# Doubles made into floats with three VectorE passes and a scaled copy, instead of four passes, a magnitude and a PSUM bank

## The chip, the cores and the metric

One core of a Trainium2 chip runs the whole program. The metric is device time in microseconds (us), the median of several executions; the profile is of one more execution. TensorE multiplies matrices, VectorE and GpSimd work elementwise, ScalarE applies functions and copies, and SyncE only issues DMAs. The profile calls them PE (with PEld for its weight loads), DVE, POOL, ACT and SP. Each engine takes its instructions strictly in the order of the program.

## The reference

An attention with a state that is corrected at every step feeds two layers of a feed-forward network. Cut to what matters here:

```
B, H, S, D = 4, 8, 768, 48              # q, k, v in float32
for t in range(S):
    y[t] = q[t] @ state
    state += beta[t] * outer(k_n[t], v[t] - k_n[t] @ state)
x = y as 3072 tokens of 384
h = x @ w_in;  g = P(h) / Q(h);  x = g @ w_out       # first MLP, 384 -> 2048 -> 384
h = x @ w_in2; g = h * tanh(softplus(h)); out = g @ w_out2
```

All four weight matrices arrive as float64. [...]

## The kernel before

**Stages.** The attention runs in chunks of 64 tokens, 12 of them (`u`), in pairs; then come 96 units of the first MLP and 96 of the second. A unit is one token group of 512 with one block of 128 of the 2048 hidden features: 9 matmuls up (L818), an elementwise chain, and 9 or 12 matmuls down (L904, L937).

**Attention.** For each chunk `prepare` loads, normalizes and transposes k and q and makes masked Gram matrices (L374 on DVE). For each pair of chunks `inverse` inverts 32 x 32 triangles in 30 steps of a product (L449) and a sum (L455): it opens with a transposition on DVE (L437) and a scaling (L440), and closes with a scaling (L459) and a transposition on DVE (L462) that writes `xt`. Four of the six inverses (chunks 3, 5, 7, 11) run on POOL, the other two (1 and 9, the first and the fifth) on DVE. `step` is the recurrence: matmuls of the pair (L509, L526, L541, L549, L564) in turns with subtractions on DVE (L517) and copies on ACT. Its L526 reads `xt`, so the recurrence of a pair starts when that pair's inverse is done.

**Weights.** `Weights.convert` makes one half of a feature block (384 doubles in each of 128 partitions) into a high and a low float32r part: 64 conversions, of which 32 (first MLP) run beside the attention, 16 in the middle of the first MLP and 16 at the start of the second. One conversion is a DMA of the doubles to `w64` (called `w` in the rows), `mag` (L665, ACT, the magnitude of the high words, to `wm`; in the second MLP L661 on DVE instead), `size` (L670 clips and L674 shifts and masks the exponent, on DVE), `sign` (L680) and `low` (L686), both on DVE, a rounding copy `out` (L693, ACT) and the remainder `rest` (L698, POOL). What the passes between read and write lies in a PSUM bank called `word` during the attention, in the `r` bank of PSUM (left over from the first MLP) in the second MLP, and in `wm` itself, in SBUF, during the first MLP.

**What sets the order.** In the attention all engines' orders are written by `Plan`: every piece of work is added with its engine, an assumed duration in ns, and the buffers it reads and writes; a list scheduler with 800 random trials of priorities picks the shortest order that it finds. The times in it are not seen by the chip, only the order is. Where the plan leaves TensorE without work it writes matmuls of zeros (`heat`, L1046) into TensorE's order, as many as the gap holds. In the two MLPs the order is written by hand in `MLP_OPS`, and `Conv.pull` deals out the steps of the conversions between units, one of `size`, `sign` and `low` at a time.

Of the kernel before, what the change touches and what calls it, by code (L numbers as in the profile page):

```python
# [9 lines left out]
F32 = mybir.dt.float32  # L10
F32R = mybir.dt.float32r
I32 = mybir.dt.int32
I64 = mybir.dt.int64
ACTF = mybir.ActivationFunctionType
ALU = mybir.AluOpType
# [7 lines left out]
TOK = 512  # L23
# [145 lines left out]
class Attention:  # L169
# [4 lines left out]
    def __init__(self, ctx, tc, q, k, v, beta, x1, spare):  # L174
        nc = self.nc = tc.nc
        self.x1 = x1
        B, H, S, D = q.shape
        self.B, self.H, self.D = B, H, D
        self.NU = S // C
        self.M = B * H // 2  # L180
        self.DP = 64
        M, DP, NU = self.M, self.DP, self.NU

        big = ctx.enter_context(tc.tile_pool(name="a_big", bufs=1))
        ps = ctx.enter_context(tc.tile_pool(name="a_ps", bufs=1, space=PSUM))

        def ring(name, n, shape, pool=big):
            return [pool.tile(shape, F32, name=f"{name}{i}") for i in range(n)]

        self.ident, = ring("ident", 1, [128, 128])  # L190
        self.mask, = ring("mask", 1, [128, 2 * C])
        self.beta, = ring("beta", 1, [128, NU // 2, HC])
        self.kn = ring("kn", self.NKN, [128, M, DP])
        self.qn = ring("qn", self.NQ, [128, M, DP])
        self.v = ring("v", self.NV, [128, M, D])
        self.kq = ring("kq", self.NT, [128, 2, M // 2, 128])
        self.gm = ring("gm", self.NT, [128, M, HC + C])
        self.su = ring("su", 2, [128, 2, M // 2, D])
        self.u = ring("u", 1, [128, M, D])
        self.r2, = ring("r2", 1, [128, M, D])  # L200
        self.lg = ring("lg", 1, [128, 2, M, HC])
        self.xs = ring("xs", 2, [128, HC, HC])
        self.lg.append(spare.rearrange("p k t -> p (k t)")[:, 0:2 * M * HC].rearrange("p (u m t) -> p u m t", u=2, m=M))
        self.xt = ring("xt", 3, [128, 2 * M, HC])
        self.tmp = ring("tmp", 2, [128, 256])
        self.yst = ring("yst", 1, [128, M, GU * C])
        self.nrm = [{n: t for n, t in zip(("ss", "n0", "r0", "n1", "ri"), ring(f"nrm{i}_", 5, [128, 2, M]))} for i in range(2)]
        self.word, = ring("word", 1, [128, 384], ps)
        self.s_all, = ring("s_all", 1, [128, 2, TOK], ps)
        self.s_ps = [self.s_all[:, i] for i in range(2)]  # L210
        self.c_ps = ring("c_ps", 2, [128, TOK], ps)
        self.t_ps = ring("t_ps", 2, [128, TOK], ps)
        self.y_ps, = ring("y_ps", 1, [128, TOK], ps)
        self.banks = 0

        def heads(t):
            t = t.rearrange("b h s d -> (b h) s d").rearrange("(a c n) s d -> a c s n d", a=2, c=2)
            return [[t[a, c] for c in range(2)] for a in range(2)]

        self.kv, self.qv, self.vv = heads(k), heads(q), heads(v)  # L220
        bv = beta.rearrange("b h s -> (b h) s").rearrange("(a m) (g u c t) -> a c u m g t", a=2, u=2, c=2, t=HC)
        self.bv = [bv[n // 4, n // 2 % 2, n % 2] for n in range(8)]
# [400 lines left out]
class Weights:  # L623
# [2 lines left out]

    LEAST = 2.0 ** -15
    MOST = 1.875 * 2.0 ** 16  # L630
    free = False
    word = None

    def __init__(self, nc, w_in, w_out, sb, kept, passing, scratch):
        self.nc, self.sb, self.kept, self.scratch = nc, sb, kept, scratch
# [10 lines left out]
    def convert(self, f, side):  # L646
        nc = self.nc
        w = {}

        def get():  # L650
            w["raw"] = self.sb.tile([128, 3, 128], I64, "w64")
            src = self.w_out[f * 128:(f + 1) * 128] if side else self.w_in[:, :, f * 128:(f + 1) * 128]
            nc.sync.dma_start(out=w["raw"], in_=src)

        def word(i):
            return w["raw"].rearrange("p k c -> p (k c)").bitcast(I32).rearrange("p (n t) -> p n t", t=2)[:, :, i]

        def mag():
            w["m"] = self.sb.tile([128, 384], I32, "wm")
            if self.free:  # L660
                nc.vector.tensor_scalar(  # L661
                    out=w["m"], in0=word(1), scalar1=0x7FFFFFFF, scalar2=None, op0=ALU.bitwise_and
                )
            else:
                nc.scalar.activation(out=w["m"].bitcast(F32), in_=word(1).bitcast(F32), func=ACTF.Abs)  # L665

        def size():
            m = w["m"]
            w["x"] = m if self.word is None else self.word.bitcast(I32)
            nc.vector.tensor_scalar(  # L670
                out=w["x"].bitcast(F32), in0=w["m"].bitcast(F32), scalar1=self.LEAST, scalar2=self.MOST,
                op0=ALU.max, op1=ALU.min,
            )
            nc.vector.tensor_scalar(  # L674
                out=w["x"], in0=w["x"], scalar1=3, scalar2=0x3FFFFFF8,
                op0=ALU.logical_shift_left, op1=ALU.bitwise_and,
            )

        def sign():
            nc.vector.scalar_tensor_tensor(  # L680
                out=w["x"], in0=word(1), scalar=-(1 << 30), in1=w["x"],
                op0=ALU.bitwise_and, op1=ALU.bitwise_or,
            )

        def low():
            nc.vector.scalar_tensor_tensor(  # L686
                out=w["m"], in0=word(0), scalar=29, in1=w["x"],
                op0=ALU.logical_shift_right, op1=ALU.bitwise_or,
            )

        def out():
            m = w["m"].bitcast(F32).rearrange("p (k c) -> p k c", k=3)
            nc.scalar.copy(out=self.tile(f)[:, 0, side], in_=m)  # L693

        def rest():
            t = self.tile(f)
            m = w["m"].bitcast(F32).rearrange("p (k c) -> p k c", k=3)
            nc.gpsimd.tensor_tensor(out=t[:, 1, side], in0=m, in1=t[:, 0, side].bitcast(F32), op=ALU.subtract)  # L698

        def done():  # L700
            if side and f in self.tag:
                self.store(f)

        return get, mag, size, sign, low, out, rest, done

    def plan(self, p, fs):

        slots = len(self.kept)
        for i, f in enumerate(fs):
            slot, late = f"w{i % slots}", LATE * i - AHEAD  # L710
            for side in range(2):
                n = 2 * i + side
                get, mag, size, sign, low, out, rest, _ = self.convert(f, side)
                raw, m = f"w64{n % 2}", f"wm{n % 2}"
                p.add("SP", 1500, get, (), [raw], more=2500, early=late)
                p.add("ACT", 560, mag, [raw], [m], early=late)
                p.add("DVE", 1160, size, [m], ["word"], early=late)
                p.add("DVE", 570, sign, [raw], ["word"], early=late)
                p.add("DVE", 570, low, [raw, "word"], [m], early=late)
                p.add("ACT", 500, out, [m], [slot], early=late)  # L720
                p.add("POOL", 1000, rest, [m], [slot], early=late)
            if f not in self.kept:
                p.add("SP", 2500, lambda f=f: self.store(f), [slot], (), more=2500, early=late)
# [224 lines left out]
def tile_delta_attention_two_mlps(  # L948
# [14 lines left out]
    nc = tc.nc  # L963
# [15 lines left out]
    ps = Ring()  # L979
# [14 lines left out]
    w1 = Weights(nc, moe_w_in, moe_w_out, sb, range(FQ), (), wd[0])  # L994
    w2 = Weights(nc, moe2_w_in, moe2_w_out, sb, (), range(DIRECT), wd[1])
# [37 lines left out]
    with ExitStack() as actx:  # L1033
        m1.xr[0] = sb.tile([128, 3, TOK], F32, "xraw")
        at = Attention(actx, tc, q, k, v, beta, x1, m1.xr[0])
# [4 lines left out]
        nc.scalar.activation(out=ab[:, 4:6], in_=ab[:, 4:6], func=ACTF.Abs)  # L1040
        zero = actx.enter_context(tc.tile_pool(name="zero", bufs=1)).tile([128, 128], F32, name="zero")
        nc.gpsimd.memset(zero, 0.0)
        w1.word = at.word

        def heat(used=False):
            nc.tensor.matmul(  # L1046
# [10 lines left out]
        late = 20000  # L1057
# [11 lines left out]
    with ExitStack() as bctx:  # L1069
# [22 lines left out]
        for i in range(n2 + max(LG.values())):  # L1092
# [10 lines left out]
            for op in LISTS[kind]:  # L1103
# [19 lines left out]
                elif op == "fw" and i in fetch_w:  # L1123
                    fetch, f = fetch_w[i]
                    fetch(f)
                elif op == "fx" and i + 8 < n2 and starts(i + 8):
                    mlp(i + 8).fetch_x(units[i + 8][0])
                elif op == "xa":
                    at_x(lambda m: m.x_hi)
                elif op == "xB":  # L1130
                    at_x(lambda m: lambda g, k: m.x_lo(g, k, "V"))
                elif op == "c" and i > n1:
                    w2.free = True
                    w2.word = w2.word or ps.tile([128, TOK], F32, "r")[:, 0:384]
                    conv.pull(CONV_RATE)
                elif op == "c" and i in calm:
                    conv.pull(6 * DIRECT * (calm.index(i) + 1) // len(calm) - conv.n)
                elif op == "f":
                    conv.flush()
# [29 lines left out]
```

## Time and profile before

| | us |
|---|---|
| median of 3 runs | 1139.59 (1138.97 to 1141.21) |
| span of the profiled execution | 1133.3 |
| of it: attention, to the first matmul of the first MLP | 0 to 317.1 |
| first MLP | 317.1 to about 718 |
| second MLP | about 718 to 1133.3 |

The profile gives the span from the first to the last instruction of its execution and no other time of it; the median of the runs is 6.3 us longer than this span. Over the span PE is busy 94%, DVE 64%, ACT 54% and POOL 47%, but these are means over three stages with different limits: DVE is busy 93% of the first MLP and 28% of the second, and POOL works in the attention, the first MLP and the first eighth of the second. So the rows further down are taken stage by stage. A busy time is the time in which an engine has an instruction under way; the idle time before an instruction is put down to what ended it.

### The profile page before, as it was taken

To read this page: it belongs to the slowest core of one execution; us is meant where nothing else is said; L and a number is where in the kernel's file an instruction comes from. 1 tells how busy PE (TensorE), PEld (TensorE's weight loads), DVE (VectorE), ACT (ScalarE), POOL (GpSimd) and SP (SyncE) were. 2 spreads that over 40 slices of the span, in tenths; PEclk is the share of its full clock that TensorE was granted. 3 is DMA by queue.
4 is the path that set the end of the run, shared out by engine and by line. 5 is a ranking of instruction groups with operands and counts; after the bars stand their busy time and mean duration, and the time that the engine had idled before them with its cause. 6 is when DMAs were issued, how large, how long until landed. Compare 5 with 4: busy or idle time off the path is not lost.

```text
span 1133.3 us, 25035 instructions
## 1 busy us (share of the span) xinstructions
PE 1068.1 (94%) x10354; PEld 933.0 (82%) x10354; DVE 720.1 (64%) x1206; ACT 611.6 (54%) x1101; POOL 538.2 (47%) x623
## 2 busy tenths in 40 slices
PE   5899899888879999999999999999999999999998
PEld 4888888778768778787887878899999998999997
DVE  5878475995669999999999999993121211212110
ACT  4415445334368888888888888743323323333322
POOL 3188878476347777787777777773000000000000
PEclk9989899988999999999999999999999999999999
DMA  7428676326585031121202036150101001010000
GB/s 139 90 54 201 163 190 172 85 59 197 178 305 204 4 108 43 50 77 52 100 17 98 14 126 249 45 190 6 56 1 56 1 1 57 1 56 1 29 1 28
DMA packets 121265, 99.23 MB, mean 88 GB/s; under 512 B 79808, under 2 KB 104512, under 8 KB 121152
## 3 DMA queue, kind: packets, MB, share of 16 engines
q1 hardware_dynamic: 120896, 97.54, 28.8%
q8 instruction: 81, 1.33, 0.5%
q14 instruction: 32, 0.26, 0.1%
q0 software_dynamic: 256, 0.10, 0.1%
HBM read 66.16 MB, written 31.46 MB: 86 GB/s over the span
## 4 chain that ended last, share of the span: by engine, by line
PE 54%; POOL 15%; ACT 11%; DVE 9%; issue 7%; DMA 2%; SPq 2%; POOLq 0%; DVEq 0%; ACTq 0%
PE h L818 21%; PE o L937 18%; POOL q L861 8%; PE o L904 4%; POOL gh L833 3%; ACT r L868 3%; POOL r L851 3%; PE y_ps L564 3%; PE c_ps L526 3%; ACT q L848 2%; ACT r L870 2%; DVE tmp L449 2%; PE c_ps L541 1%; PE c_ps L509 1%; PE s_all L549 1%
## 5 line engine op out<-in xcount | busy, mean ns | idle before, releaser
L818 PE MATMUL h<-x,w 128*128 128x512 f32 x1728 | 429.1, 393 | 7.5 <-DVE s L877 3.5
L818 PEld LDWEIGHTS h<-x,w 128*128 128x128 f32 x1728 | 321.3, 188 | 76.6 <-DVE s L877 8.7
L833 DVE TENSOR_TENSOR gh<-g,gh 128x512 fp32r<-128x512 f32 x80 | 55.4, 693 | 283.0 <-ACT g L928 274.3
L904 PE MATMUL o<-gh,w 128*128 128x512 f32 x864 | 213.5, 391 | 4.9 <-ACT ev L1026 4.9
L937 PE MATMUL o<-w,gh 128*128 128x384 f32 x1152 | 216.9, 337 | 0.0
L937 PEld LDWEIGHTS o<-w,gh 128*128 128x128 f32 x1152 | 204.7, 188 | 8.1
L904 PEld LDWEIGHTS o<-gh,w 128*128 128x128 f32 x864 | 161.7, 188 | 41.0 <-ACT ev L1026 7.8
L923 ACT ACTIVATE gh<-h 128x512 fp32r<-128x512 f32 x96 | 57.6, 600 | 229.0 <-PE h L818 229.0
L833 POOL TENSOR_TENSOR gh<-g,gh 128x512 fp32r<-128x512 f32 x112 | 145.1, 1296 | 23.9 <-ACT g L928 21.4
L861 POOL TENSOR_TENSOR q<-q,r 128x512 f32<-128x512 f32 x96 | 124.6, 1298 | 65.7 <-ACT r L855 61.2
L868 ACT ACTIVATE r<-q,cst 128x512 f32<-128x512 f32 x96 | 66.4, 691 | 52.5 <-POOL q L861 52.5
L884 DVE SCALAR_TENSOR_TENSOR q<-q,r 128x512 f32<-128x512 f32 x96 | 65.2, 679 | 15.0 <-ACT r L870 14.7
L698 POOL TENSOR_TENSOR w<-wm,w 128x384 fp32r<-128x384 f32 x48 | 49.6, 1035 | 52.6 <-ACT w L693 52.4
L857 ACT ACTIVATE s<-h,ab 128x512 f32<-128x512 f32 x96 | 74.3, 774 | 0.0
L877 DVE SCALAR_TENSOR_TENSOR s<-s,ab,h 128x512 f32<-128x512 f32 x96 | 71.8, 748 | 3.4
L888 DVE SCALAR_TENSOR_TENSOR r<-s,ab,r 128x512 f32<-128x512 f32 x96 | 71.7, 746 | 0.0
L875 DVE TENSOR_TENSOR s<-s,h 128x512 f32<-128x512 f32 x96 | 65.4, 681 | 6.0 <-ACT s L857 6.0
L893 DVE SCALAR_TENSOR_TENSOR g<-q,r 128x512 f32<-128x512 f32 x96 | 65.9, 687 | 3.3
L455 POOL TENSOR_TENSOR xs<-xs,tmp 128x30 f32<-128x30 f32 (+14 forms) x120 | 62.1, 518 | 9.4
L449 POOL TENSOR_TENSOR tmp<-xs 128x30 f32<-128x30 f32 (+14 forms) x120 | 58.3, 486 | 7.0
L829 ACT CAST gh<-g 128x512 fp32r<-128x512 f32 x96 | 59.7, 622 | 0.0
L851 POOL TENSOR_SCALAR r<-q,ab 128x512 f32<-128x512 f32 x54 | 42.1, 780 | 34.8 <-ACT q L848 34.8
(125 smaller groups left out, 1397.0 us busy)
## 6 DMA issues: line engine op xcount, KB each, us to landing
w<-w SPq DMA_DIRECT2D x36, 768.0 KB, 7.3
w<-in_moe_w_in_dram SPq DMA_DIRECT2D x32, 384.0 KB, 4.0
w<-in_moe_w_out_dram SPq DMA_DIRECT2D x32, 384.0 KB, 3.4
xraw<-x SPq DMA_DIRECT2D x36, 256.0 KB, 3.9
w<-wt SPq DMA_DIRECT2D x8, 768.0 KB, 3.8
kn<-in_k_dram SPq DMA_DIRECT2D x48, 96.0 KB, 3.7
qn<-in_q_dram SPq DMA_DIRECT2D x48, 96.0 KB, 3.4
v<-in_v_dram SPq DMA_DIRECT2D x48, 96.0 KB, 3.5
```

The lines of the kernel that those rows point to most:

```text
L449: eng.tensor_tensor(out=tv, in0=ls[:, j, j + 1:HC].unsqueeze(1).to_broadcast([128, j, n]), in1=xs[:, 0:j, j:j + 1].to_broadcast([128, j, n ...
L818: self.nc.tensor.matmul(out=self.st[i]["h"], lhsT=self.w.t[f][:, a, 0, k], rhs=self.x[g][:, b, k], start=(n == 0), stop=(n == 8),)
L833: (nc.gpsimd if engine == "P" else nc.vector).tensor_tensor(out=s["gh"][:, 1], in0=s["g"], in1=s["gh"][:, 0].bitcast(F32), op=ALU.subtract)
L851: nc.gpsimd.tensor_scalar(out=s["r"], in0=s["q"], scalar1=k["b1"], scalar2=k["b0"], op0=ALU.mult, op1=ALU.add)
L857: nc.scalar.activation(out=s["s"], in_=s["h"], func=ACTF.Identity, scale=k["a3"], bias=k["a2"])
L861: nc.gpsimd.tensor_tensor(out=s["q"], in0=s["q"], in1=s["r"], op=ALU.mult)
L868: nc.scalar.activation(out=s["r"], in_=s["q"], func=ACTF.Ln, bias=k["c"])
L877: nc.vector.scalar_tensor_tensor(out=s["s"], in0=s["s"], scalar=k["a1"], in1=s["h"], op0=ALU.add, op1=ALU.mult)
L888: nc.vector.scalar_tensor_tensor(out=s["r"], in0=s["s"], scalar=k["a0"], in1=s["r"], op0=ALU.add, op1=ALU.mult)
L893: nc.vector.scalar_tensor_tensor(out=s["g"], in0=s["q"], scalar=2.0, in1=s["r"], op0=ALU.subtract, op1=ALU.mult, reverse0=True)
L904: self.nc.tensor.matmul(out=self.acc[g][d], lhsT=self.w.t[f][:, a, 1, d], rhs=self.st[i]["gh"][:, b], start=(first and n == 0), stop=(last ...
L937: self.nc.tensor.matmul(out=self.acc[g][t][:, 0:384], lhsT=self.st[i]["gh"][:, a, t * 128:(t + 1) * 128], rhs=self.w.t[f][:, b, 1].rearran ...
```

## The change

`mag` becomes a scaled copy: ACT multiplies the high word, read as a float, by 2^-112, which moves the exponent by the difference of the two formats' biases and keeps the sign (in the second MLP DVE does the same with a multiplication). `size` is then one shift by three to the left, from `wm` into the high words of the raw doubles themselves, nothing is clipped and nothing masked; `sign` takes the sign bit from `wm`, and `low` is as it was. The bank `word` and the use of the `r` bank fall away: all that the three passes read and write is in SBUF, in every stage. In the plan `size` is entered with 360 instead of 1160 ns, and the buffers that the passes claim are named anew.

```
-        self.word, = ring("word", 1, [128, 384], ps)
...
-    LEAST = 2.0 ** -15
-    MOST = 1.875 * 2.0 ** 16
+    SCALE = 2.0 ** -112
...
         def mag():
             w["m"] = self.sb.tile([128, 384], I32, "wm")
+            m, src = w["m"].bitcast(F32), word(1).bitcast(F32)
             if self.free:
-                nc.vector.tensor_scalar(
-                    out=w["m"], in0=word(1), scalar1=0x7FFFFFFF, scalar2=None, op0=ALU.bitwise_and
-                )
+                nc.vector.tensor_scalar(out=m, in0=src, scalar1=self.SCALE, scalar2=None, op0=ALU.mult)
             else:
-                nc.scalar.activation(out=w["m"].bitcast(F32), in_=word(1).bitcast(F32), func=ACTF.Abs)
+                nc.scalar.activation(out=m, in_=src, func=ACTF.Copy, scale=self.SCALE)
 
         def size():
-            m = w["m"]
-            w["x"] = m if self.word is None else self.word.bitcast(I32)
+            w["x"] = word(1)
             nc.vector.tensor_scalar(
-                out=w["x"].bitcast(F32), in0=w["m"].bitcast(F32), scalar1=self.LEAST, scalar2=self.MOST,
-                op0=ALU.max, op1=ALU.min,
-            )
-            nc.vector.tensor_scalar(
-                out=w["x"], in0=w["x"], scalar1=3, scalar2=0x3FFFFFF8,
-                op0=ALU.logical_shift_left, op1=ALU.bitwise_and,
+                out=w["x"], in0=w["m"], scalar1=3, scalar2=None, op0=ALU.logical_shift_left
             )
 
         def sign():
             nc.vector.scalar_tensor_tensor(
-                out=w["x"], in0=word(1), scalar=-(1 << 30), in1=w["x"],
+                out=w["x"], in0=w["m"], scalar=-(1 << 31), in1=w["x"],
                 op0=ALU.bitwise_and, op1=ALU.bitwise_or,
             )
...
-                p.add("DVE", 1160, size, [m], ["word"], early=late)
-                p.add("DVE", 570, sign, [raw], ["word"], early=late)
-                p.add("DVE", 570, low, [raw, "word"], [m], early=late)
+                p.add("DVE", 360, size, [m], [raw], early=late)
+                p.add("DVE", 570, sign, [m], [raw], early=late)
+                p.add("DVE", 570, low, [raw], [m], early=late)
```

The new costs make the scheduler write another order for the whole attention. In the changed program `size` is L665, `sign` L670 and `low` L676, `rest` L688, and other lines of the attention stand one lower than before (L436 for L437, L461 for L462, L516 for L517, L525 for L526), `heat` is L1035. The conversions keep their places in the orders of the two MLPs, one pass shorter each. Three places:

DVE ahead of the transposition that opens the first inverse (`yst<-lg`), the program before:

```order
L374 TENSOR_TENSOR gm_138<-c_ps_169,mask_120 128x384
L670 TENSOR_SCALAR word_166<-wm 128x384
L674 TENSOR_SCALAR word_166<-word_166 128x384
L680 SCALAR_TENSOR_TENSOR word_166<-w_351,word_166 128x384
L686 SCALAR_TENSOR_TENSOR wm<-w_351,word_166 128x384
L670 TENSOR_SCALAR word_166<-wm 128x384
L674 TENSOR_SCALAR word_166<-word_166 128x384
L437 STREAM_TRANSPOSE yst_155<-lg_147 128x1024
```

and the changed one:

```order
L373 TENSOR_TENSOR gm_138<-c_ps_168,mask_120 128x384
L316 TENSOR_REDUCE nrm_0_156<-gm_142 128x16
L326 TENSOR_SCALAR nrm_0_156<-nrm_0_156 128x32
L436 STREAM_TRANSPOSE yst_155<-lg_147 128x1024
L373 TENSOR_TENSOR xraw<-t_ps_170,mask_120 128x128
L373 TENSOR_TENSOR xraw<-t_ps_169,mask_120 128x128
L373 TENSOR_TENSOR gm_139<-t_ps_170,mask_120 128x384
L373 TENSOR_TENSOR gm_139<-t_ps_169,mask_120 128x384
L665 TENSOR_SCALAR w_450<-wm 128x384
```

One and a half conversions went from ahead of the first inverse to behind it, and two sums of squares (L316) with a small L326 came forward.

DVE at the end of the fifth inverse, which it runs itself (`xs_148` to `xt_151`), the program before:

```order
L517 TENSOR_TENSOR r_146<-r_146,c_ps_168 128x384
L449 TENSOR_TENSOR tmp_153<-xs_148 128x84
L455 TENSOR_TENSOR xs_148<-xs_148,tmp_153 128x28x3
L449 TENSOR_TENSOR tmp_153<-xs_148 128x58
L455 TENSOR_TENSOR xs_148<-xs_148,tmp_153 128x29x2
L670 TENSOR_SCALAR word_166<-wm 128x384
L674 TENSOR_SCALAR word_166<-word_166 128x384
L449 TENSOR_TENSOR tmp_153<-xs_148 128x30
L455 TENSOR_TENSOR xs_148<-xs_148,tmp_153 128x30
L459 TENSOR_TENSOR xs_148<-xs_148,beta_121 128x1024
L462 STREAM_TRANSPOSE xt_151<-xs_148 128x32x32
```

and a piece of the changed one, a little further ahead in the same inverse:

```order
L454 TENSOR_TENSOR xs_148<-xs_148,tmp_153 128x23x8
L676 SCALAR_TENSOR_TENSOR wm<-w_3442 128x384
L448 TENSOR_TENSOR tmp_153<-xs_148 128x168
L454 TENSOR_TENSOR xs_148<-xs_148,tmp_153 128x24x7
L448 TENSOR_TENSOR tmp_153<-xs_148 128x150
L454 TENSOR_TENSOR xs_148<-xs_148,tmp_153 128x25x6
L516 TENSOR_TENSOR r_146<-v_130,c_ps_168 128x384
L676 SCALAR_TENSOR_TENSOR wm<-w_3524 128x384
L448 TENSOR_TENSOR tmp_153<-xs_148 128x130
L454 TENSOR_TENSOR xs_148<-xs_148,tmp_153 128x26x5
```

Conversions moved forward, into this inverse: between the transposition that closes the fourth inverse (L462, `xt_150`) and the one that closes the fifth there are 2 passes of conversions before and 10 now.

PE where the recurrence of the fifth pair begins (its first L526 that reads `xt_151`), the program before:

```order
L564 MATMUL y_ps_172<-kq_132,su_144 48x64 x16
L509 MATMUL c_ps_168<-su_143,kq_133 64x48 x16
L564 MATMUL y_ps_172<-gm_138,u_145 48x64 x16
L526 MATMUL c_ps_169<-r_146,xt_151 32x48 x16
L526 MATMUL c_ps_168<-r_146,xt_151 32x48 x16
```

and the changed one:

```order
L563 MATMUL y_ps_171<-gm_138,u_145 48x64 x16
L508 MATMUL c_ps_167<-su_143,kq_133 64x48 x16
L563 MATMUL y_ps_171<-kq_133,su_143 48x64 x16
L1035 MATMUL s_all_166<-ident_119,zero 128x128 x24
L525 MATMUL c_ps_168<-r_146,xt_151 32x48 x16
L525 MATMUL c_ps_167<-r_146,xt_151 32x48 x16
```

24 matmuls of zeros now stand ahead of it, where there were none.

## Rows read from the trace of the kernel before

**Rows 1.** Busy us of each engine in stretches: start:end, length, engine (instructions), clock.
```profile
core 0: us, PE busy (x) PEld busy (x) DVE busy (x) ACT busy (x) POOL busy (x), PEclk, DMA share, GB/s
217.50:254.00 36.50, 30.65 (x935) 28.39 (x936) 34.30 (x63) 10.59 (x21) 20.48 (x36) 0.91 0.19 47
254.00:287.60 33.60, 28.49 (x907) 26.63 (x904) 20.04 (x36) 12.90 (x27) 20.99 (x34) 0.85 0.59 171
317.10:717.90 400.80, 389.27 (x1691) 315.35 (x1692) 373.65 (x554) 343.07 (x582) 298.77 (x258) 1.00 0.28 101
717.90:1133.30 415.40, 410.62 (x2055) 371.11 (x2053) 116.01 (x183) 136.89 (x259) 44.15 (x38) 1.00 0.11 36
```
**Rows 2.** PE's waits, 317 to 720 us: us in total, times, longest.
```profile
PE o L904 <- ACT ev L1026: 4.9, 5, 1.4
PE h L818 <- DVE s L877: 3.5, 6, 1.7
PE h L818 <- DVE q L884: 3.0, 1, 3.0
```
**Rows 3.** Passes of conversions by line: ns min/median/max, first and last start.
```profile
L674 DVE TENSOR_SCALAR wm<-wm x16: 359/708/1061, 352.6 to 681.2; 128x384 int32<-128x384 int32 x16
L661 DVE TENSOR_SCALAR wm<-w x15: 347/564/1494, 726.9 to 770.1; 128x384 int32<-128x384 int32 x15
L680 DVE SCALAR_TENSOR_TENSOR word<-w,word x32: 503/561/578, 31.2 to 315.9; 128x384 int32<-128x384 int32 x32
L680 DVE SCALAR_TENSOR_TENSOR wm<-w,wm x16: 551/690/1359, 356.3 to 684.8; 128x384 int32<-128x384 int32 x16
L686 DVE SCALAR_TENSOR_TENSOR wm<-w,wm x16: 642/920/1358, 364.3 to 688.7; 128x384 int32<-128x384 int32 x16
```
**Rows 4.** Timeline (start, us, instruction) of POOL and DVE where both read SBUF.
```profile
227.76 2.43 POOL L440 TENSOR_TENSOR xs<-xs,beta 128x1024 f32<-128x1024 f32 x1 [13.03 <-DVE xs L437]
228.01 2.45 DVE L455 TENSOR_TENSOR xs<-xs,tmp 128x238 f32<-128x238 f32 x1
...
406.74 1.30 POOL L833 TENSOR_TENSOR gh<-g,gh 128x512 fp32r<-128x512 f32 x1 [0.37 <-ACT gh L829]
407.09 1.36 DVE L680 SCALAR_TENSOR_TENSOR wm<-w,wm 128x384 int32<-128x384 int32 x1
```
**Rows 5.** Timeline of POOL, the same two steps in its first and its last inverse.
```profile
61.53 0.41 POOL L449 TENSOR_TENSOR tmp<-xs 128x130 f32<-128x130 f32 x1
72.68 0.60 POOL L449 TENSOR_TENSOR tmp<-xs 128x238 f32<-128x238 f32 x1
...
233.88 0.41 POOL L449 TENSOR_TENSOR tmp<-xs 128x130 f32<-128x130 f32 x1
245.25 0.61 POOL L449 TENSOR_TENSOR tmp<-xs 128x238 f32<-128x238 f32 x1
```
**Rows 6.** POOL: a remainder and the third inverse's closing (timeline), its longest waits, 27:317.
```profile
34.84 1.00 POOL L698 TENSOR_TENSOR w<-wm,w 128x384 fp32r<-128x384 f32 x1 [4.34 <-ACT w L693]
...
212.82 1.91 POOL L459 TENSOR_TENSOR xs<-xs,beta 128x1024 f32<-128x1024 f32 x1
...
POOL w L698 <- ACT w L693: 50.6, 16, 7.6
```
**Rows 7.** Chain of waits: start, us, piece; DVE up to the opening of POOL's first inverse.
```profile
53.13 0.40 DVE tmp L449
...
53.96 1.88 DVE xs L437
```
**Rows 8.** PE where the fifth pair begins (timeline), and its matmuls of zeros (groups).
```profile
256.43 1.55 PE L526 MATMUL c_ps<-r,xt 32*32 32x48 f32 x64 [1.87 <-DVE r L517]
...
L1046 PE MATMUL s_all<-ident,zero 128*128 128x128 f32 x158 | 21.3, 288 | 0.0
```
**Rows 9.** Timeline of PE at the start of the first MLP.
```profile
317.13 4.42 PE L818 MATMUL h<-x,w 128*128 128x512 f32 x18 [0.90 <-DVE wm L686]
...
331.40 2.34 PE L818 MATMUL h<-x,w 128*128 128x512 f32 x9 [1.75 <-DVE s L877]
```

More of the change, by code (lines that the diff above doesn't have):

```diff
@@ L623 @@
 class Weights:
-    LEAST = 2.0 ** -15
-    MOST = 1.875 * 2.0 ** 16
+    SCALE = 2.0 ** -112
     free = False
-    word = None
     def __init__(self, nc, w_in, w_out, sb, kept, passing, scratch):
@@ L1042, in tile_delta_attention_two_mlps @@
         nc.gpsimd.memset(zero, 0.0)
-        w1.word = at.word
         def heat(used=False):
@@ L1133, in tile_delta_attention_two_mlps @@
                     w2.free = True
-                    w2.word = w2.word or ps.tile([128, TOK], F32, "r")[:, 0:384]
                     conv.pull(CONV_RATE)
```

## The prediction

> **What bounds the kernel now.** I read the busy time by stretches first [rows 1], because the three stages have different limits. In the second MLP PE is busy 410.6 of 415.4 us and DVE 116.0: only PE counts there. In the first MLP PE is busy 389.3 of 400.8 us, but DVE is close behind with 373.7, so the next view is what PE waited for in that stage [rows 2]: 4.9 us on ACT's copies of accumulators, 6.5 us in seven waits on DVE. No more than these can a faster DVE give back there. In the attention no engine is full: between the closing of the fourth and of the fifth inverse (217.5 to 254.0 us) DVE is busy 34.3 of 36.5 us, and in the next stretch 20.0 of 33.6 [rows 1]. So the attention is bound by a chain that changes engines: POOL's inverses one after the other, DVE's own fifth inverse, and the recurrence on PE, which may start a pair only when its `xt` is there. The conversions are not in that chain by themselves. They count by where they stand in DVE's and POOL's order, and by what they do to the instructions beside them.
>
> **What a pass costs now and then.** Before, four passes with an operand in PSUM take 0.56 us each and never over 0.58 (L680 on `word` [rows 3]), 2.24 us for a conversion. Afterwards three passes lie wholly in SBUF, as they did in the first MLP, where the same kinds have medians of 0.71, 0.69 and 0.92 us, together 2.32, and minima of 0.36, 0.55 and 0.64, together 1.55 [rows 3]. The cause stands in the timeline: a DVE instruction with both inputs in SBUF started 0.25 us after POOL's 2.43 us scaling and took 2.45 us, and an L680 beside a POOL subtraction took 1.36 us [rows 4]. Such a DVE instruction ends only after POOL's has ended. In the attention POOL's instructions are shorter (0.41 to 0.61 us [rows 5]) but come one behind the other. I take 2.1 us for a conversion, nearer to the medians; the bounds are 1.55 and 2.32. So DVE is relieved by 0.1 us for each of the 32 conversions of the attention, while the new plan counts on 1.50 us for it, 0.74 less than the 2.24. The shift also writes every second word; the one row with that stride (L661, reading it) has 0.35 us at least [rows 3], and were it slower, up to 0.56 us, it would stay inside these bounds.
>
> **(a) The start.** Up to the opening of POOL's first inverse (53.96 us, straight behind steps of DVE's first inverse [rows 7]) DVE has 6 passes before and 1 afterwards, but 2 more inverse steps of two times 0.40 us and one small instruction of about 0.2 us: -6 x 0.56 + 0.36 + 1.6 + 0.2 = **-1.2 us**. At best the 3.4 us of the passes, at worst 0.
>
> **(b) POOL's queue.** From the opening of its first inverse to the closing of its third, POOL runs 18 remainders before and 20 afterwards; each takes 1.00 us [rows 6]: +2.0 us. What the passes in SBUF cost POOL the trace doesn't show for 384 elements. Nearest: the same nine steps of an inverse took 11.15 us with DVE in PSUM (61.53 to 72.68) and 11.37 beside DVE's own steps of some 200 elements (233.88 to 245.25) [rows 5], 0.22 us more for about 17 DVE instructions. 20 conversions with two two-input passes each lie between 0.5 us by that and 22 us if POOL waits 0.55 us each time; the passes are twice as long as those steps, so I take 0.05 us each, +2.0 us. POOL's waits for conversions (50.6 us in 16 waits [rows 6]) I leave as they are: the DVE part of a conversion hardly shortens. Together **+4.0 us** (-6 to +22).
>
> **(c) The fifth pair.** Between the closings of the fourth and the fifth inverse DVE was full [rows 1], and it gets 8 passes more: 8 x 0.36 to 0.92 = +2.9 to +7.4 us. PE shows the same from its side: it waited 1.87 us for that inverse [rows 8], and its order now holds 24 matmuls of zeros there; 79 of them took 21.3 us [rows 8] (the row counts each twice), 0.27 us each, so 6.5 us, which PE runs whether it would have to wait or not. 6.5 - 1.9 = **+4.6 us**. In the whole attention 20 more are in the order (253, not 233).
>
> **(d) The end of the attention.** Behind the last inverse 6 passes stand on DVE and 4 remainders on POOL, where 26 and 8 stood. So the first matmul of the first MLP no longer waits 0.9 us for the last conversion [rows 9], and DVE's subtractions in the last pair meet fewer passes: another 1.0 us (0 to 3). **-1.9 us.** What is late next is the recurrence itself, which PE's own matmuls fill.
>
> **(e) The MLPs.** In the first MLP 16 passes of 0.71 us leave DVE, 11.3 of its 373.7 us. PE can get back at most its waits on DVE, and of their 6.5 us the one of 3.0 and the longest of the others, 1.75 at 331.4 us [rows 2, 9], come ahead of the first conversion there (its L674 from 352.6 us [rows 3]). Of the 1.7 us left I take half: **-0.8 us** (0 to -1.7). In the second the passes leave PSUM, and beside POOL's subtractions they will take about the 2.3 us that four took: DVE has the same load, and PE reads a block's weights only some units after they are made. Cost 0; without that cover some 2 us.
>
> ACT's scaled copy reads and writes what the magnitude did: nothing.
>
> **The sum.** -1.2 + 4.0 + 4.6 - 1.9 - 0.8 = +4.7 us on the span of 1133.3, so 1138.0; with the 6.3 us between the span and the median of the runs, **1144.3 us**.
>
> **Rivals.** *The passes run free.* If most of them find POOL idle (it does idle, 50.6 us, for these very conversions [rows 6]), each comes in 1.55 us, and remainders arrive up to 0.7 us sooner: 16 waits x 0.7 = 11 us, of which I count 8; with (a) -1.2, two remainders +2, (c) +4.6, (d) -3.9 and (e) -1.7 that is -8.2: 1131.4 us. For it: a shift right behind POOL's instruction can take 0.36 us. Against: the medians of the first MLP, and 24 fixed matmuls in PE's order.
>
> *The terms cancel.* The six passes at the start come through whole (-3.4), the port costs POOL nothing (+2.0 for two remainders), (c) to (e) as above: +0.5, 1140.1 us.
>
> *POOL is held for whole passes.* Slower by far: each of the three passes keeps POOL's next instruction waiting for its own length, 20 x (0.36 + 0.55 + 0.55) = 29 us up to the third inverse. POOL's waits for conversions would hide about half of it; with +15 for the 2.0 of the port the sum is +17.7: 1157.3 us. It decides once POOL's cadence in an inverse stretches by more than 0.2 us at a pass; rows 5 speak against it, with shorter DVE instructions. The Trainium skill, "SBUF — State Buffer", section "Who interferes with whom", states this rule: VectorE with two SBUF inputs, or in a two-port mode, and GpSimd exclude each other for a whole instruction, and the one that comes second blocks fully. By that rule this rival is the forecast, at 1157.3 us; rows 4 agree for a DVE that comes second, rows 5 show hardly any cost to POOL.
>
> **How the numbers follow.** The forecast has 0.42, the free passes 0.28, the cancelling 0.22, the held POOL 0.08. 0.2%, or 2.3 us, is about what a measurement of this kernel can tell from no change. Faster: 0.28 and a little of the cancelling, 0.30. Slower: the held POOL and most of the forecast, 0.47. The same: 0.23. The forecast alone runs from 1140 to 1152 (port 0.5 to 8 us, (c) 2.9 to 7.4). The range for 8 in 10 leaves out the held POOL and the far end of the free passes: 1131 to 1152.
>
> **What would show it.** Passes in the attention with medians near 0.7 us, not 0.4 to 0.55; POOL's third inverse closing 2 to 5 us later than at 214.7 [rows 6]; the first L526 of the fifth pair behind 24 fills or later; the first MLP starting at about 319 us, not 317.1, without a wait on a conversion, and lasting about 1 us less. It would be wrong if the opening of POOL's first inverse moved by much more than 1 us, if POOL's waits for conversions fell by half, or if TensorE's clock (0.91 and 0.85 in two stretches [rows 1]) rose or fell with the new order.

## The result, and the profile after

| | before | after |
|---|---|---|
| median, same chip, 4 executions each | 1139.28 us (1137.06 to 1141.21) | 1150.05 us (1145.61 to 1150.47) |
| ratio, 95% interval | | 1.0106 (1.0069 to 1.0143) |
| span of the profiled execution | 1133.3 us | 1148.6 us |
| first matmul of the first MLP | 317.1 us | 332.9 us |
| from there to the end | 816.2 us | 815.7 us |

The changed kernel is slower, by 1.1% in the ratio and by 10.8 us, or 0.9%, between the medians. A ratio, here and below, is of the fast executions alone (those within 1.5% of the fastest of their kernel) and is not the quotient of the medians beside it. The two profiled spans lie 15.3 us apart, and all of it is in the attention. In runs that give both numbers the time is about 2 us longer than the span, not 6.3, so the execution profiled before lies some 4 us under its median.

Stretches of the changed kernel, columns as in [rows 1]. The first two lie between the closing transpositions of the fourth and fifth, and of the fifth and sixth inverse; then the two MLPs.

```profile
232.90:275.70 42.80, 35.50 (x1018) 33.51 (x1016) 40.42 (x73) 15.66 (x32) 26.01 (x40) 0.92 0.47 132
275.70:304.80 29.10, 25.30 (x814) 24.39 (x814) 14.89 (x24) 11.14 (x24) 20.57 (x32) 0.77 0.54 160
...
332.90:733.00 400.10, 389.24 (x1690) 316.12 (x1690) 368.67 (x538) 343.08 (x581) 296.85 (x257) 1.00 0.28 101
733.00:1148.60 415.60, 410.93 (x2056) 371.14 (x2054) 122.80 (x167) 136.58 (x260) 47.77 (x38) 1.00 0.11 36
```

Against [rows 1] the DVE-bound stretch has grown from 36.5 to 42.8 us, the one behind it has shrunk from 33.6 to 29.1, and the MLPs have kept their lengths.

What four passes cost in the attention before and what three cost now: groups by line, 27 us to the end of the attention (busy us in all, mean ns of one | idle before them), first before, then after.

```profile
L674 DVE TENSOR_SCALAR word<-word 128x384 int32<-128x384 int32 x32 | 18.1, 566 | 1.1
L680 DVE SCALAR_TENSOR_TENSOR word<-w,word 128x384 int32<-128x384 int32 x32 | 17.9, 558 | 0.7
L670 DVE TENSOR_SCALAR word<-wm 128x384 f32<-128x384 f32 x32 | 17.8, 556 | 28.4 <-ACT wm L665 27.8
L686 DVE SCALAR_TENSOR_TENSOR wm<-w,word 128x384 int32<-128x384 int32 x32 | 17.7, 554 | 2.7
```

```profile
L670 DVE SCALAR_TENSOR_TENSOR w<-wm,w 128x384 int32<-128x384 int32 x32 | 27.5, 859 | 1.0
L676 DVE SCALAR_TENSOR_TENSOR wm<-w 128x384 int32<-128x384 int32 x32 | 24.6, 774 | 1.4
L665 DVE TENSOR_SCALAR w<-wm 128x384 int32<-128x384 int32 x32 | 20.3, 633 | 15.4 <-ACT wm L661 15.2
```

Four passes took 71.5 us of DVE, three take 72.4. A quarter of the instructions is gone and none of the time: 2.27 us for a conversion, where the plan now counts 1.50 (360, 570 and 570 ns).

The same hold-up from POOL's side: the products and sums of its four inverses, groups as above, before and after.

```profile
L455 POOL TENSOR_TENSOR xs<-xs,tmp 128x30 f32<-128x30 f32 (+14 forms) x120 | 62.1, 518 | 9.4
L449 POOL TENSOR_TENSOR tmp<-xs 128x30 f32<-128x30 f32 (+14 forms) x120 | 58.3, 486 | 7.0
```

```profile
L454 POOL TENSOR_TENSOR xs<-xs,tmp 128x30 f32<-128x30 f32 (+14 forms) x120 | 67.8, 565 | 9.4
L448 POOL TENSOR_TENSOR tmp<-xs 128x30 f32<-128x30 f32 (+14 forms) x120 | 65.3, 544 | 7.0
```

The same 240 instructions (120 steps of a product and a sum) take 133.1 us, not 120.4. The timeline of the changed kernel (start, us, instruction, in brackets what was waited for) shows one place, in the order of time, ahead of the third inverse's end:

```profile
209.86 0.56 ACT L661 ACTIVATE wm<-w 128x384 f32<-128x384 f32 x1 [3.02 <-DMA w<-in_moe_w_in_dram]
...
210.45 0.36 DVE L665 TENSOR_SCALAR w<-wm 128x384 int32<-128x384 int32 x1 [2.02 <-ACT wm L661]
...
210.85 0.56 DVE L670 SCALAR_TENSOR_TENSOR w<-wm,w 128x384 int32<-128x384 int32 x1
...
212.51 0.35 DVE L341 RECIPROCAL nrm<-nrm 128x32 f32<-128x32 f32 x1
...
213.00 3.02 POOL L393 TENSOR_TENSOR kn<-kn,nrm 128x768 f32<-128x768 f32 x2 [3.39 <-DVE nrm L341]
...
213.42 1.27 DVE L665 TENSOR_SCALAR w<-wm 128x384 int32<-128x384 int32 x1
...
214.73 1.71 DVE L670 SCALAR_TENSOR_TENSOR w<-wm,w 128x384 int32<-128x384 int32 x1
...
225.99 1.91 POOL L458 TENSOR_TENSOR xs<-xs,beta 128x1024 f32<-128x1024 f32 x1
```

Two things are to be seen. DVE stood 2.02 us at a conversion whose doubles had not landed; behind that pass in its order came the norm (L341), for which POOL waited 3.39 us with its inverse unfinished. That is order. Then a shift and a sign pass, begun 0.4 and 1.7 us after POOL's two scalings began, took 1.27 and 1.71 us instead of 0.36 and 0.56. That is the place of the operands. The closing of the third inverse is at 225.99 us; in [rows 6] it is at 212.82.

And the fifth pair on PE (timeline), answering [rows 8]:

```profile
267.82 3.62 PE L1035 MATMUL s_all<-ident,zero 128*128 128x128 f32 x31
277.75 2.53 PE L525 MATMUL c_ps<-r,xt 32*32 32x48 f32 x58 [6.30 <-DVE xt L461]
...
332.85 4.42 PE L808 MATMUL h<-x,w 128*128 128x512 f32 x18
340.34 5.03 PE L808 MATMUL h<-x,w 128*128 128x512 f32 x14 [3.07 <-DMA w<-w]
```

The matmuls of zeros were over by 271.4 us (the first row shows only the last 31 of their 48 records, two to a matmul); PE then waited 6.30 us for the fifth inverse itself. The first MLP no longer waits for a conversion [rows 9], but later for a fetched weight.

### The profile page after: what moved, and what is told of

Its sections match the earlier page's. It is cut to its first block, busy times and chain, and to the rows that moved or that the text cites. A ratio compares the mean times of both kernels' runs of the same rounds, so it can differ in the third digit from the quotient of the medians.

```text
span 1148.6 us, 25024 instructions
## 1 busy us (share of the span) xinstructions
PE 1077.8 (94%) x10394; PEld 945.3 (82%) x10394; DVE 721.4 (63%) x1142; ACT 611.4 (53%) x1101; POOL 554.6 (48%) x623
## 4 chain that ended last, share of the span: by engine, by line
PE 46%; POOL 17%; DVE 12%; ACT 12%; issue 8%; DMA 3%; SPq 2%; POOLq 0%; DVEq 0%; ACTq 0%
PE h L808 17%; PE o L927 15%; POOL q L851 8%; POOL gh L823 4%; POOL r L841 3%; ACT r L858 3%; PE c_ps L525 3%; PE y_ps L563 3%; ACT q L838 2%; ACT r L860 2%; DVE w L670 2%; SPq L237 2%; PE o L894 2%; PE s_all L548 2%; DVE wm L676 2%
## 5 line engine op out<-in xcount | busy, mean ns | idle before, releaser
L823 POOL TENSOR_TENSOR gh<-g,gh 128x512 fp32r<-128x512 f32 x112 | 147.6, 1319 | 5.4 <-ACT g L918 2.9
L688 POOL TENSOR_TENSOR w<-wm,w 128x384 fp32r<-128x384 f32 x48 | 51.2, 1067 | 55.3 <-ACT w L683 54.0
L454 POOL TENSOR_TENSOR xs<-xs,tmp 128x30 f32<-128x30 f32 (+14 forms) x120 | 67.8, 565 | 9.4
L448 POOL TENSOR_TENSOR tmp<-xs 128x30 f32<-128x30 f32 (+14 forms) x120 | 65.3, 544 | 7.0
L676 DVE SCALAR_TENSOR_TENSOR wm<-w 128x384 int32<-128x384 int32 x64 | 59.5, 932 | 1.8
L670 DVE SCALAR_TENSOR_TENSOR w<-wm,w 128x384 int32<-128x384 int32 x64 | 59.3, 927 | 1.4
```

The source lines that it names most:

```text
L454: eng.tensor_tensor(out=xs[:, 0:j, j + 1:HC], in0=xs[:, 0:j, j + 1:HC], in1=tv, op=ALU.add)
L670: nc.vector.scalar_tensor_tensor(out=w["x"], in0=w["m"], scalar=-(1 << 31), in1=w["x"], op0=ALU.bitwise_and, op1=ALU.bitwise_or,)
L676: nc.vector.scalar_tensor_tensor(out=w["m"], in0=word(0), scalar=29, in1=w["x"], op0=ALU.logical_shift_right, op1=ALU.bitwise_or,)
L823: (nc.gpsimd if engine == "P" else nc.vector).tensor_tensor(out=s["gh"][:, 1], in0=s["g"], in1=s["gh"][:, 0].bitcast(F32), op=ALU.subtract)
```

## The experiments

Two causes were left over by the traces. **Place**: passes in SBUF and POOL hold each other up. **Order**: the changed kernel runs another order, found by a planner that was told 360, 570 and 570 ns for passes that take 633, 859 and 774. The recorded expectations call them theory P and theories O, C and S.

### The same order, the operand's place alone

First the three passes of the change with the plan's old entries, so the old order:

```
-                p.add("DVE", 360, size, [m], [raw], early=late)
-                p.add("DVE", 570, sign, [m], [raw], early=late)
-                p.add("DVE", 570, low, [raw], [m], early=late)
+                p.add("DVE", 1160, size, [m], ["word"], early=late)
+                p.add("DVE", 570, sign, [raw], ["word"], early=late)
+                p.add("DVE", 570, low, [raw, "word"], [m], early=late)
```

> The three passes of the change, wholly in SBUF, but the planner is given the old entries (1160, 570, 570 ns and the buffer word), so that PE, ACT, POOL and SP run exactly the order of before and DVE the same less one pass of each conversion in the attention. Theory P (passes in SBUF and POOL hold each other up): the stretch of POOL's inverses stays, the third closes at 222 to 230 us (214.7 before, 227.9 after), the first MLP starts at 326 to 333 us, 1145 to 1150 us. Theory O (the new order costs the time, whatever the operands): the third inverse closes at 212 to 216 us, the first MLP starts at 314 to 318 us, 1135 to 1139 us. Theory C (the planner was given too short costs): as O.

Then the same, with the word between the passes in PSUM (`w["x"] = word(1) if self.word is None else self.word.bitcast(I32)`, the bank allocated as before):

> The same as the kernel with the old order and three passes, but what stands between the passes lies in PSUM (the bank word is back). Theory P: POOL's third inverse closes at 211 to 215 us, the first MLP starts at 313 to 317 us, and one pass of 0.56 us less in each conversion gives 1135 to 1139 us, 8 to 13 us below the same order with SBUF. Theory O: within 2 us of the same order with SBUF, 1135 to 1139 us for both.

And the kernel before, four passes, with the word in `wm`:

```
-        w1.word = at.word
```

> The kernel before, its order and its four passes, but with what stands between the passes in wm, in SBUF, and not in the PSUM bank: only the operand's place is changed, in the attention alone. If passes in SBUF and POOL's steps hold each other up by what the kernel with three passes in the old order showed (POOL's steps 128.6 us in all, not 120.7): steps of 127 to 133 us in all, the third inverse closing 5 to 9 us later than 212.8 us, the first MLP starting 2 to 6 us later than 317.1, and 1136 to 1142 us. If the place costs nothing: the third inverse within 1.5 us of 212.8 and 1134 to 1137 us.

| order of before | median us | ratio (95%) | POOL's steps us | third closing | first MLP |
|---|---|---|---|---|---|
| before: four passes, PSUM | 1136.2 and 1136.4 | | 120.4 | 212.8 | 317.1 |
| three, SBUF | 1137.10 | 0.9984 (0.9943 to 1.0026) | 128.7 | 218.0 | 318.8 |
| three, PSUM | 1139.15 | 1.0038 (0.9999 to 1.0077) | 120.7 | 212.6 | 322.0 |
| four, SBUF | 1140.70 | 1.0049 (1.0008 to 1.0090) | 129.9 | 214.7 | 315.9 |

POOL's steps, groups by line, of three passes in SBUF, three in PSUM, and four in SBUF:

```profile
L454 POOL TENSOR_TENSOR xs<-xs,tmp 128x30 f32<-128x30 f32 (+14 forms) x120 | 65.1, 542 | 9.4
L448 POOL TENSOR_TENSOR tmp<-xs 128x30 f32<-128x30 f32 (+14 forms) x120 | 63.6, 530 | 7.0
```

```profile
L455 POOL TENSOR_TENSOR xs<-xs,tmp 128x30 f32<-128x30 f32 (+14 forms) x120 | 62.3, 519 | 9.4
L449 POOL TENSOR_TENSOR tmp<-xs 128x30 f32<-128x30 f32 (+14 forms) x120 | 58.4, 487 | 7.0
```

```profile
L455 POOL TENSOR_TENSOR xs<-xs,tmp 128x30 f32<-128x30 f32 (+14 forms) x120 | 65.9, 549 | 9.4
L449 POOL TENSOR_TENSOR tmp<-xs 128x30 f32<-128x30 f32 (+14 forms) x120 | 64.0, 534 | 7.0
```

The place has a price on POOL in both pairs, 8 us with three passes and 9.5 with four, and one on DVE, where the passes took 67.9 us in SBUF and 53.4 in PSUM with three, 85.5 and 71.5 with four. In the old order little of it reaches the end. Three passes in SBUF closed the third inverse 5.2 us later than before and started the first MLP 1.7 us later; four in SBUF 1.9 us later, where 5 to 9 were expected, and 1.3 us earlier. The profiled execution with four in SBUF was a quick one, 5 us under its median, so its starts say less than its time. The times lie within half a per cent of before; for four in SBUF the interval leaves out 1, so there the place did cost something, 0.1 to 0.9%. Theory P asked for 1145 to 1150 us for three in SBUF and gets 1137.1, at most 0.3% above before by its interval. So the three passes of the change, hold-up and all, lose next to nothing in the old order; the loss needs the new one.

The removed pass by itself, three passes in PSUM, gained nothing either. Why is open: they closed the third inverse when before did and yet started the first MLP 4.9 us later, and the granted clock over the attention (27 us to the first MLP) was 0.87 there, 0.92 before. The pass may have been off the path, or the clock may have taken back what it gave.

### What the planner was told

The new entries with durations near the measured ones:

```
-                p.add("DVE", 360, size, [m], [raw], early=late)
-                p.add("DVE", 570, sign, [m], [raw], early=late)
-                p.add("DVE", 570, low, [raw], [m], early=late)
+                p.add("DVE", 600, size, [m], [raw], early=late)
+                p.add("DVE", 900, sign, [m], [raw], early=late)
+                p.add("DVE", 900, low, [raw], [m], early=late)
```

> The changed kernel with 600, 900 and 900 ns in the planner in place of 360, 570 and 570, about what the passes took beside POOL. Theory P: POOL's steps stay stretched (mean 0.54 and 0.56 us), and 1144 to 1150 us. Theory C: an order that counts on the true durations brings most of the loss back, 1137 to 1141 us.

Three passes in PSUM with an order of their own (560, 570 and 570 ns and the buffer `word`):

> Three passes with PSUM between them, and the planner given 560, 570 and 570 ns, near what such passes took before; so an order of its own, near that of the changed kernel in load. Theory P: 1133 to 1140 us, the passes at 0.56 us each, mean of POOL's inverse steps near 0.49 and 0.52 us as before. Theory O: an order made for three passes costs the time, 1144 to 1150 us, with POOL's steps as short as before.

The long durations gave 1140.97 us, ratio 1.0042 (1.0011 to 1.0072): POOL's steps stretched as in the changed kernel (130.0 us), and still over half of the loss is gone. PSUM with a new order gave 1137.82 us, 1.0025 (0.9993 to 1.0057). So these two new orders cost little, both made with durations near the truth.

One order proves little, since the planner's search is random. So its own arithmetic was run over each order a second time, with 470, 900 and 900 ns, which sum to the measured 2.27 us, and with those of POOL's entries that are under 1000 ns 10% longer, among them only 32 of the 120 steps of its inverses, where the expectations speak of POOL's steps without limit ("counted", to ACT's last copy, some 1 us ahead of the end that the planner believes in; for passes in PSUM and for before with the entries as they are). And the search was started elsewhere:

```
-        kinds, rng = sorted(set(self.kinds)), random.Random(0)
+        kinds, rng = sorted(set(self.kinds)), random.Random(2)
```

The changed kernel again, and with starts 1 and 2:

> The changed kernel once more, on the chip of the others. All theories: 1146 to 1152 us, its first MLP starting at 328 to 334 us.

> The changed kernel with another start of the planner's random search (1, not 0): the same passes, the same 360, 570 and 570 ns, another order. The planner believes in an end of the attention 4.7 us earlier than for the changed kernel (289.1, not 293.7 us of its own count); the same count over this order with the measured 470, 900 and 900 ns and POOL's steps 10% longer gives 298.5 us, where it gives 306.1 for the changed kernel and 290.4 for before with its own durations. Theory C (an order made for passes that are too short loses when they take longer): 7.5 us less than the changed kernel and 8 more than before, 1141 to 1146 us. Theory S (orders scatter, whatever durations they are made for): anything between 1130 and 1150 us, as likely below before as above.

> The changed kernel with start 2 of the planner's search, and 360, 570 and 570 ns as it has. The planner believes in 284.0 us, 9.7 us better than for the changed kernel and 7.4 better than for before; counted with 470, 900 and 900 ns and POOL's steps 10% longer the order ends at 294.9 us, 4.6 later than before's. Theory C (made for passes that are too short): 1138 to 1143 us. Theory S (only the quality of the order as the planner sees it counts): 1127 to 1133 us.

Start 2 with 470, 900 and 900 ns in the plan:

> The same passes and the same start 2, but the planner has 470, 900 and 900 ns, what the passes took in the changed kernel. It believes in 285.6 us, about as much as with the short durations, and counted with POOL's steps 10% longer the order ends at 286.6. Theory C: 4 to 9 us less than the kernel with start 2 and short durations, 1131 to 1136 us. Theory S: within 2 us of it.

| three passes in SBUF | planner believes | counted | first MLP | median us | ratio to before (95%) |
|---|---|---|---|---|---|
| 360, 570, 570, start 0 (the change) | 293.7 | 306.1 | 331.9 | 1152.63 | 1.0165 (1.0114 to 1.0215) |
| 360, 570, 570, start 1 | 289.1 | 298.5 | 319.7 | 1142.08 | 1.0062 (1.0033 to 1.0091) |
| 360, 570, 570, start 2 | 284.0 | 294.9 | 321.3 | 1140.73 | 1.0041 (1.0002 to 1.0080) |
| 600, 900, 900, start 0 | 292.8 | 292.5 | 321.1 | 1140.97 | 1.0042 (1.0011 to 1.0072) |
| 470, 900, 900, start 2 | 285.6 | 286.6 | 309.4 | 1131.36 | 0.9952 (0.9920 to 0.9984) |
| before (four, PSUM), start 0 | 291.4 | 290.4 | 317.1 | about 1136 | |

What the planner believes does not order these times: 284.0 with short durations gave 1140.7, 285.6 with true ones 1131.4. What is counted does: it lies 12.4, 9.4 and 10.9 us beyond the belief where the durations were short, within 1 us where they were near the truth. It does so only roughly: by the trace start 1 began the first MLP earlier than start 2, by the count later.

The count also hangs on how POOL's steps are lengthened. By the trace of the changed kernel all 120 steps with the gaps ahead of them took 149.5 us, where the plan's entries sum to 144.6, so 3.4% more. With all of them 3.4% longer the same arithmetic gives 306.1, 299.2, 295.2, 294.6 and 288.9 us in the order of the table, not far from it. With all of them 10% longer it gives 309.0, 305.8, 299.9, 303.9 and 298.3: the five keep the sequence of their times, but each lies 11 to 17 us beyond its belief, short durations or true, and the last would end 7.9 us behind before, where it ran 5 us ahead.

Start 2 with true durations is the one version that beat both kernels, by 0.5% against before; it was picked as the best-counted of six starts (286.6 to 299.6 us), so part of that is the draw. First matmul of the first MLP in the two kernels with start 2 (timeline), short durations first:

```profile
321.34 4.38 PE L808 MATMUL h<-x,w 128*128 128x512 f32 x18
```

```profile
309.35 4.37 PE L808 MATMUL h<-x,w 128*128 128x512 f32 x18
```

POOL waiting in its third inverse, same two kernels in the same order (us in all, times, longest):

```profile
POOL w L688 <- ACT w L683: 4.6, 2, 4.2
POOL kn L393 <- PE t_ps L364: 2.1, 1, 2.1
POOL xs L439 <- DVE xs L436: 1.5, 1, 1.5
```

```profile
POOL xs L439 <- DVE xs L436: 3.7, 1, 3.7
POOL kn L393 <- DVE nrm L341: 3.3, 2, 2.7
```

With true durations POOL does not wait for a conversion there at all. But its waits in all fall only from 8.2 to 7.0 us, so most of the 12.0 us at the first MLP must come from elsewhere in the order, which these rows don't show. Its steps are as stretched as ever (132.3 us): the gain is made beside the hold-up, not by removing it.

### Where the count stops telling

Two orders that the count liked best, and one with more matmuls of zeros (`WINDOW, IDLE = 3400, 0` instead of 600):

> The kernel before with another start of the search (5): the planner's count ends 4.1 us earlier (287.3, not 291.4 us). If that count tells orders apart where its durations are right: 1130 to 1134 us, the first MLP starting at 311 to 315 us. If it doesn't: 1135 to 1140 us or more.

> Three passes with PSUM between them, 560, 570 and 570 ns in the planner, and another start of the search (4), with which the planner's count ends at 284.4 us, 7.0 us before that of the kernel before (291.4) and 11.8 before that of the same kernel with the first start (296.1). If three passes without the hold-up and an order with true durations bring what the change was to bring: 1127 to 1133 us. If the end of the attention is set by something that the count doesn't see (TensorE's clock, PE's own matmuls): 1134 to 1139 us.

> The kernel with three passes in PSUM and start 4, with the planner's allowance for an idle PE set to 0, not 600 ns, which puts 244 matmuls of zeros into PE's order, not 201; nothing else moves. If the granted clock takes back what that order gains (0.877 over its attention): the clock over the attention at 0.90 or more and 1128 to 1132 us. If not the clock: 1134 to 1138 us, the fills taking what they give.

Before with start 5 gave 1134.02 us, 1.0005 (0.9972 to 1.0038); PSUM with start 4 1134.37, 0.9993 (0.9966 to 1.0020); with more fill 1133.00, 0.9969 (0.9935 to 1.0003). None can be told from before, though the first two were counted 4 and 7 us shorter and began the first MLP at 313.6 and 316.6 us. In the profiled execution the granted clock over the attention went from 0.88 to 0.91 with more fill, and the first MLP started at 314.3, not 316.6. Whether it is the clock that takes these gains back is open: the interval holds both answers.

## Why the prediction came out so

The forecast was 1144.3 us with 1131 to 1152 around it, slower the likeliest; measured 1150.05. The sign and the range held. The sum was short by only 5.8 us against the median, and in part that is luck: the terms must be read against the two spans, which differ by 15.3 us where the sum had 4.7, and 4.8 us of that error vanish because the 6.3 us between span and median, which the forecast carried over, shrank to 1.5.

| step | forecast us | measured us |
|---|---|---|
| (a) POOL's first opening | -1.2 | -1.1 |
| (b) to the third closing | +4.0 | +14.3 |
| from there to the fourth `xt`, on DVE | none | +2.2 |
| (c) fourth to fifth `xt` | +4.6 | +6.3 |
| fifth to sixth `xt` | none | -4.5 |
| (d) sixth `xt` to the first MLP | -1.9 | -1.5 |
| (e) MLPs | -0.8 | -0.4 |

**What a pass costs** was mis-sized at first: 2.1 us was taken, the median of the first MLP's passes being the nearest rows; 2.27 was measured, inside the bounds of 1.55 to 2.32. So DVE was not relieved by 0.1 us a conversion, but by nothing.

**(b) is the step that failed**, in two terms. The port: from the first opening to the third closing POOL's 180 steps took 99.0 us, 89.9 before, +9.1 where 2.0 were taken. Rows 5, on which that rested, set POOL beside DVE steps of some 200 elements; the passes have 384. Two inputs in SBUF, which two of the three passes have, those steps had as well; what else than the length made a pass dearer than the 0.05 us taken is not shown. And POOL's idle time, which the forecast left as it was, grew from 26.9 to 30.3 us. What it waited for there (us in all, times, longest), before and after:

```profile
POOL w L698 <- ACT w L693: 12.7, 6, 4.5
POOL kn L394 <- DMA x<-yst: 1.6, 1, 1.6
```

```profile
POOL w L688 <- ACT w L683: 10.3, 6, 3.6
POOL kn L393 <- DVE nrm L341: 5.3, 2, 3.4
POOL kn L393 <- issue: 2.1, 1, 2.1
```

The waits for conversions did stay about what they were; the new ones are for norms that stand behind passes on DVE. The two more remainders cost the 2.0 us that were forecast (2.2), the scalings of k came out 0.9 us shorter, and 0.5 us is small work. The plan's 1.50 us for a conversion was noted in the forecast and then not used: it was read as a fact about the plan, not as the reason why the whole order would run late.

**(c)** was near in size by luck, for the wrong reason. PE did not wait behind 24 fills; it waited 6.30 us for an inverse that DVE, busy 40.4 of 42.8 us, finished late. The 1.87 us of before that the forecast took off were, by their row, a wait for a subtraction (`r`, L517) that DVE ran behind that inverse, not for `xt`. The -4.5 us of the next stretch, which nothing in the forecast stood for, go with a DVE that is busy 14.9 us there, not 20.0 [rows 1]: 16 passes stand there and not 24, the others earlier.

**(d)** held: the wait of [rows 9] is gone. **(e)** held in the total, not in its working: three passes took 41.3 us in the first MLP where four took 48.9, so 7.6 us left DVE and not 11.3. PE's waits on DVE fell from 6.5 us [rows 2] to 1.3, and PE lost 3.1 us to a weight transfer and 1.5 more to ACT's copies instead:

```profile
PE o L894 <- ACT ev L1016: 6.4, 5, 1.5
PE h L808 <- DMA w<-w: 3.1, 1, 3.1
PE h L808 <- DVE s L867: 1.3, 2, 0.9
```

In the second MLP the passes with two inputs cost more than forecast, 36.0 us for two where PSUM had 17.8, and DVE had room for it (122.8 of 415.6 us busy).

**The rivals.** *The passes run free* is refuted by the 2.27 us. *POOL is held for whole passes* had the right sign of mechanism and too much of it: 12.7 us over 96 passes is 0.13 us a pass, where it decided from 0.2. The Trainium skill, "SBUF — State Buffer", section "Who interferes with whom", says that a VectorE instruction with two SBUF inputs, or in a two-port mode, and a GpSimd instruction that reads SBUF shut each other out for a whole instruction. The pass of 1.71 us beside POOL's scalings, which has two inputs in SBUF, agrees with it for a VectorE that comes second; the shift of 1.27 us has one input, and whether it ran in a two-port mode no run here shows. But the hold-up summed over POOL's steps is a quarter of the passes' undisturbed lengths (32 times 0.36 + 0.55 + 0.55 is 46.7 us), and in the old order it hardly reached the end.

**The clock** was named as something that would upset the forecast, and it fell: 0.92 over the attention before, 0.88 after (columns as in [rows 1]).

```profile
27.00:317.10 290.10, 253.96 (x6440) 233.68 (x6432) 217.04 (x435) 120.57 (x240) 186.22 (x296) 0.92 0.55 138
27.00:332.90 305.90, 264.42 (x6475) 245.79 (x6465) 215.04 (x401) 120.46 (x239) 200.91 (x297) 0.88 0.51 132
```

It cannot be the whole cause: three passes in SBUF in the old order ran their attention at 0.88 as well and began the first MLP 1.7 us later than before, not 15.7; start 1 ran at 0.92 and start 0 with long durations at 0.93, and both were slower than before all the same. How much of the rest it took is not separated.

What stays open is the split between short durations and chance in the changed kernel's own order: of six starts with short durations the counted ends run from 294.9 to 306.1 us, and start 0 is the worst of them. In each of the six the count lies 9 to 13 us beyond the belief; the rest is the draw. By the same count the six starts with 470, 900 and 900 ns end 0.1 to 13.9 us earlier than their twins, 6.5 in the mean (4.8 with all of POOL's steps 3.4% longer), and start 0 ends at 299.6, 6.5 us earlier. By that, less than half of the changed kernel's 15.7 us would go with the durations and the rest with the draw. That order was not run. A run that keeps the changed kernel's order and shortens only its passes was not made: in that order two conversions overlap on DVE, for which one PSUM bank has no room.

## What to carry to other kernels

Where a planner writes the order, an instruction's assumed duration is part of the program: run its arithmetic over its own order with durations measured beside the other engines before the kernel is timed. Here that count had +15.7 us against before for the changed order, and the trace had +15.7; so close a match is chance, since for the other four orders of the table count and trace lie 0.3 to 5.6 us apart. A pass saved is worth only its busy time in place: three passes that share SBUF with POOL cost DVE what four in PSUM had cost. Such a count tells orders 10 us apart, not 4.

## What was not expected of the hardware

The hold-up between DVE and POOL is far less than if each pass held POOL up for its whole length. With only the operand's place changed, 128 DVE passes moved into SBUF, half of them with two inputs, stretched 240 POOL steps from 120.4 to 129.9 us, while single passes went up to 2.15 us.

Executions of one program differ by more than most of its versions do, along with the clock that they were granted: 28 of 31 executions of before, on one chip, ran spans from 1125.7 us at a mean clock of 0.978 to 1141.7 us at 0.965, while the medians of all versions but the changed one lie between 1131.4 and 1142.1 us. The three passes in PSUM in the old order ran at 0.969 in the median, those in SBUF at 0.9725, and the ones in PSUM were not quicker.
